# A two-layer MLP behind a dynamic convolution: the fifth product of each slice with 96 stationary columns for 128

## The chip, the core and the metric

The kernel runs on one core of one Trainium2 chip. The metric is the device time of one execution in microseconds (us). The core has five engines: TensorE (PE, with a row of its own for weight loads, PEld), VectorE (DVE), ScalarE (ACT), GpSimd (POOL) and SyncE (SP), which issues most DMAs.

## What is computed

The reference, cut to what matters. A softmax over 7 taps makes weights for a causal convolution along the sequence, in 8 groups of 24 features; its result of 8192 tokens x 192 features goes through two MLPs without biases, 192 to 2048 to 192 each. Everything is in float32; inputs come as float64 bits.

```python
def _attn_ref(x, weight_gen):            # x: 2 x 4096 x 192, weight_gen: 2 x 4096 x 8 x 7
    w = softmax(weight_gen, axis=-1)     # written out in the reference
    x_unf = x_pad[:, idx, :].reshape(B, S, K, H, group)
    out = np.einsum('bshk,bskhg->bshg', w, x_unf)
    return out.reshape(B, S, D)

def _moe_ref(x, w_in, w_out):            # first MLP
    r = np.maximum(x @ w_in, 0.0)
    return (r * r) @ w_out

def _moe2_ref(x, w_in, w_out):           # second MLP
    h = x @ w_in
    return (h * (1.0 / (1.0 + np.exp(-1.702 * h)))) @ w_out
```

## The kernel before

The 8192 tokens are cut into 16 blocks of N = 512; the 2048 hidden features (FF) into 16 slices of 128, which are worked on in 8 pairs, q = 0 to 7. A step is (l, j, q): layer l, block j, pair of slices q. For each step `mm_in` makes the hidden values h of the two slices, ScalarE applies the activation (g), and `mm_out` adds their part of the output into PSUM, where it collects over all q.

To keep float32 precision at the rate of the fp32r type, each operand is split into a high part (rounded to fp32r) and a low part (what is left, again in fp32r), and a product is made as a sum of products of parts. g becomes gh (a cast on ScalarE, line 387) and gl (g - gh, a subtraction on VectorE, line 393). The weights of the second product, `wo`, have for each slice f a row of 2 x 192 columns: high parts of features 0 to 127, then high parts of the 64 features past 128 (at column P = 128), then low parts of these 64 (at 192), then low parts of features 0 to 127 (at C_LA = 256). `SECOND` (line 396) lists the five products of a slice as (output a, first column of wo, part of g):

- (0, 0, 0): gh with the high parts of features 0 to 127, into output 0
- (0, C_LA, 0): gh with their low parts, into output 0
- (1, P, 0): gh with 128 columns from column 128, that is, the high and the low parts of features 128 to 191 side by side, into output 1
- (0, 0, 1): gl with the high parts of features 0 to 127, into output 0
- (1, P, 1): gl with the same 128 columns from 128 on, into output 1; of these only the 64 of the high parts matter, the other 64 are the product of two low parts

Output 1 holds the two halves for the features past 128 on partitions 0 to 63 and 64 to 127; they are added later by a swap through DMA (`t_swap`) and an addition.

In all but the first two blocks of layer 0, a product is issued as two matmuls, on rows 0 to 63 and 64 to 127 of the operands (`HALVES`), into PSUM tiles of their own: p00 and p01 for output 0, p10 and p11 for output 1. These are the forms 64*128. In blocks 0 and 1 of layer 0 (`whole`) it is one matmul on all 128 rows. In the last step of a block, q = 7, the ten products of its two slices are sorted by output, so that output 0 is complete before output 1. `start` marks the matmul that opens a sum in PSUM, `stop` the last.

The order of the work is written out by hand. Steps alternate on PE as mm_in of step n + 2, then mm_out of step n. In each turn of the loop gl is made, then PE's part issued, then the planned side work, then gh. gh and gl have two buffers each. Behind mm_out of a block's last step stands `sum_task`, in which ScalarE copies p00 and p10 (line 431) and VectorE adds p01 and p11 (line 432). `transposed` (line 345) and `t_turn` (line 519) transpose on PE at block borders.

Of the kernel before, what the change touches and what calls it, by code (L numbers as in the profile page):

```python
# [17 lines left out]
def kernel(  # L18
# [15 lines left out]
    P = 128  # L34
# [8 lines left out]
    NF = FF // P  # L43
    NQ = NF // 2
# [30 lines left out]
    wih, wil, wo = [], [], []  # L75
    DM = D - P
# [6 lines left out]
    C_HM, C_LM, C_LA = P, P + DM, P + 2 * DM  # L83
# [281 lines left out]
    p_t = {}  # L365
# [27 lines left out]
        nc.vector.tensor_sub(gl, g, f32(gh))  # L393
        g_t[l, j, q] = gh, gl

    SECOND = [(0, 0, 0), (0, C_LA, 0), (1, P, 0), (0, 0, 1), (1, P, 1)]

    def mm_out(l, j, q):

        g = g_t.pop((l, j, q))  # L400
        whole = l == 0 and j < 2
        parts = [(slice(0, P), j)] if whole else [(HALVES[i], i) for i in range(2)]
        if q == 0:
            p_t[l, j] = {
                (a, i): ps_p.tile([P, N], F32, tag=f"p{a}{i}", name=f"p{a}{i}_{l}_{j}")
                for a in range(2) for _, i in parts
            }
        ops = [(e, o, *op) for e in range(2) for o, op in enumerate(SECOND)]
        if q == NQ - 1:

            ops.sort(key=lambda op: op[2])
        for e, o, a, c, n in ops:
            f = 2 * q + e
            for rows, i in parts:
                nc.tensor.matmul(  # L415
                    out=p_t[l, j][a, i], lhsT=wo[l][rows, f, c:c + P], rhs=g[n][rows, e, :],
                    start=(f == 0 and o in (0, 2)), stop=(f == NF - 1 and o >= 3),
                )

    def sum_task(l, j, hold):  # L420

        def f():
            s = hold["s"] = s_p.tile([P, 2, N], F32, tag="s", name=f"s{l}_{j}")
            p = p_t.pop((l, j))
            if len(p) == 2:
                for a in range(2):
                    nc.scalar.copy(s[:, a, :], p[a, j])
                return
            t = s_p.tile([P, 2, N], F32, tag="s", name=f"t{l}_{j}")
            for a in range(2):  # L430
                nc.scalar.copy(t[:, a, :], p[a, 0])  # L431
                nc.vector.tensor_add(s[:, a, :], p[a, 1], t[:, a, :])  # L432

        return f
# [116 lines left out]
    second_step = [4 * (n // 2) + 6 + n % 2 if n < WHOLE - LAG else 2 * (n + LAG) + 1 for n in range(len(pairs))]  # L551
    steps = {i: (mm_in, n) for n, i in enumerate(first_step)}
    steps |= {i: (mm_out, n) for n, i in enumerate(second_step)}
    assert len(steps) == 2 * len(pairs)
    first, done = {}, {}
# [84 lines left out]
    for s in range(3, TP // SB):  # L640
        i = first[0, s * SB // TB - 1] - 7
        plan(softmax(s), (i - 8, i, i + 1, i + 2, i + 3))
    for n in range(2 * NQ):
        kind = (InChunk, OutChunk)[n % 2]
        i = 4 * NQ + 7.5 + n * 4.0
# [16 lines left out]
    for n, i in enumerate(first_step):  # L662
        i = second_step[n - LAG] if LAG <= n < WHOLE else i + 1
# [3 lines left out]
    with tc.manual_schedule():  # L667
        for i in range(-PRE, 2 * (len(pairs) + LAG) + 8):
# [3 lines left out]
            if i in steps:  # L672
                f, n = steps[i]
# [36 lines left out]
```

## Time and profile before

| | us |
|---|---|
| median of 3 runs | 1166.42 |
| lowest and highest | 1166.27, 1166.82 |
| span of the profiled execution, first to last instruction | 1163.6 |
| median less span | 2.8 |
| PE busy in that span | 1146.5 |
| ACT busy | 780.1 |
| DVE busy | 677.6 |

The profile is of one execution; its span is what its rows add up to, and the time of a run lies some us above it. A busy time is the time in which at least one instruction of the engine runs. Ends of matmuls are modelled, and neighbours overlap, so for PE the distance from start to start says more than a duration. The granted clock is given as a share of full speed.

### The profile page before, as it was taken

To read this page: it belongs to the slowest core of one execution; us is meant where nothing else is said; L and a number is where in the kernel's file an instruction comes from. 1 tells how busy PE (TensorE), PEld (TensorE's weight loads), DVE (VectorE), ACT (ScalarE), POOL (GpSimd) and SP (SyncE) were. 2 spreads that over 40 slices of the span, in tenths; PEclk is the share of its full clock that TensorE was granted. 3 is DMA by queue.
4 is the path that set the end of the run, shared out by engine and by line. 5 is a ranking of instruction groups with operands and counts; after the bars stand their busy time and mean duration, and the time that the engine had idled before them with its cause. 6 is when DMAs were issued, how large, how long until landed. Compare 5 with 4: busy or idle time off the path is not lost.

```text
span 1163.6 us, 23632 instructions
## 1 busy us (share of the span) xinstructions
PE 1146.5 (99%) x10248; PEld 1109.3 (95%) x10248; DVE 677.6 (58%) x792; ACT 780.1 (67%) x851; POOL 17.6 (2%) x26
## 2 busy tenths in 40 slices
PE   6999999999999999999999999999999999999998
PEld 4777899999999999999999999999999999999998
DVE  7998899794564636555474554746455343343342
ACT  3877888876767667675767757677575765555554
POOL 1000010010000000000000000000000000000000
PEclk9999999999999999999999999999999999999999
DMA  8503452532120121210211120121210110110110
GB/s 208 171 1 84 108 143 64 139 76 60 46 62 9 39 58 41 62 37 10 58 50 53 37 60 8 50 58 33 62 37 10 24 42 19 37 37 11 32 37 28
DMA packets 35576, 64.04 MB, mean 55 GB/s; under 512 B 5268, under 2 KB 21138, under 8 KB 35472
## 3 DMA queue, kind: packets, MB, share of 16 engines
q1 hardware_dynamic: 32640, 59.25, 18.3%
q0 software_dynamic: 2304, 3.15, 1.7%
q8 instruction: 80, 1.31, 0.5%
q14 instruction: 24, 0.20, 0.1%
q10 hardware_dynamic: 528, 0.13, 0.0%
HBM read 30.13 MB, written 6.29 MB: 31 GB/s over the span
## 4 chain that ended last, share of the span: by engine, by line
PE 97%; DVE 1%; ACT 1%; DMA 1%; issue 0%; SPq 0%; DVEq 0%
PE p L415 50%; PE h L374 45%; PE tx L345 1%; DMA xt<-in_x_dram 1%; DVE pr L290 1%; PE u L519 0%; PE sumi L107 0%; ACT g L380 0%; DVE xs L325 0%; ACT xs L324 0%; DVE early_us L157 0%; ACT g L381 0%; PE sumo L107 0%; DVE early_us L161 0%; DVE early_us L156 0%
## 5 line engine op out<-in xcount | busy, mean ns | idle before, releaser
L393 DVE TENSOR_TENSOR gl<-g,gh 128x1024 fp32r<-128x1024 f32 x256 | 313.2, 1224 | 327.7 <-ACT gh L387 326.0
L415 PE MATMUL p<-gh,wo 64*128 64x512 f32 (+1 forms) x2976 | 472.0, 387 | 0.6 <-ACT wo L217 0.6
L374 PE MATMUL h<-xs,wih 64*128 64x512 f32 x3072 | 460.3, 389 | 0.4 <-DVE xs L325 0.2
L415 PEld LDWEIGHTS p<-gh,wo 64*128 64x128 f32 (+1 forms) x2976 | 349.6, 184 | 10.1 <-issue 2.5
L374 PEld LDWEIGHTS h<-xs,wih 64*128 64x128 f32 x3072 | 345.0, 184 | 10.3 <-issue 1.8
L415 PE MATMUL p<-gl,wo 64*128 64x512 f32 (+1 forms) x1984 | 354.8, 386 | 0.0
L387 ACT CAST gh<-g 128x1024 fp32r<-128x1024 f32 x256 | 268.7, 1050 | 79.4 <-PE p L415 76.9
L415 PEld LDWEIGHTS p<-gl,wo 64*128 64x128 f32 (+1 forms) x1984 | 236.3, 184 | 4.4
L374 PE MATMUL h<-xs,wil 64*128 64x512 f32 x1536 | 228.9, 387 | 0.1
L383 ACT ACTIVATE g<-h 128x1024 f32<-128x1024 f32 x128 | 131.7, 1029 | 144.8 <-PE h L374 132.2
L380 ACT ACTIVATE g<-h 128x1024 f32<-128x1024 f32 x128 | 131.7, 1029 | 104.5 <-PE h L374 103.0
L374 PEld LDWEIGHTS h<-xs,wil 64*128 64x128 f32 x1536 | 174.5, 184 | 4.3 <-DVE wil L203 0.6
L381 ACT ACTIVATE g<-g 128x1024 f32<-128x1024 f32 x128 | 135.8, 1061 | 4.1
L290 DVE TENSOR_TENSOR pr<-xt,wg 128x768 f32<-128x768 f32 x112 | 104.9, 951 | 2.2 <-DMA xt<-in_x_dram 2.2
L302 DVE TENSOR_TENSOR pr<-pr,pr 128x768 f32<-128x768 f32 x84 | 80.1, 954 | 1.0
L432 DVE TENSOR_TENSOR s<-p,t 128x512 f32<-128x512 f32 x60 | 40.3, 689 | 55.7 <-ACT t L431 55.6
L325 DVE TENSOR_TENSOR xs<-s,xs 128x1024 fp32r<-128x1024 f32 x16 | 19.6, 1226 | 39.5 <-ACT xs L324 39.5
L431 ACT COPY t<-p 128x512 f32<-128x512 f32 x60 | 33.7, 584 | 12.7 <-PE p L415 12.7
L325 DVE TENSOR_TENSOR xs<-tx,xs 128x1024 fp32r<-128x1024 f32 x16 | 19.3, 1204 | 30.0 <-ACT xs L324 30.0
L345 PEld LDWEIGHTS tx<-ident,pr 64*128 64x128 f32 x448 | 19.5, 150 | 12.7 <-DVE pr L290 10.9
L345 PE MATMUL tx<-ident,pr 64*128 64x64 f32 x448 | 19.6, 237 | 10.7 <-DVE pr L290 10.5
L324 ACT CAST xs<-tx 128x1024 fp32r<-128x1024 f32 x16 | 16.2, 1011 | 12.0 <-PE tx L345 11.9
(73 smaller groups left out, 273.1 us busy)
## 6 DMA issues: line engine op xcount, KB each, us to landing
xs<-xs SPq DMA_DIRECT2D x128, 128.0 KB, 2.4
xt<-in_x_dram SPq DMA_DIRECT2D x14, 960.0 KB, 5.0
out_dram<-o SPq DMA_DIRECT2D x15, 384.0 KB, 2.8
w<-s SPq DMA_DIRECT2D x32, 128.0 KB, 2.3
early_raw<-in_moe_w_in_dram SPq DMA_DIRECT2D x16, 192.0 KB, 5.1
early_raw<-in_moe_w_out_dram SPq DMA_DIRECT2D x8, 384.0 KB, 4.0
ri<-in_moe_w_in_dram SPq DMA_DIRECT2D x16, 192.0 KB, 3.5
ro<-in_moe_w_out_dram SPq DMA_DIRECT2D x8, 384.0 KB, 3.2
```

The source lines that it names most:

```text
L290: nc.vector.tensor_mul(pr, hold["x"][:, k:k + TB, :].rearrange("p t (h g) -> p t h g", h=H), wg_t[s][:, t0:t0 + TB, :, k:k + 1].to_broadca ...
L302: nc.vector.tensor_add(hold["p", 0], hold["p", 0], p)
L325: lambda: nc.vector.tensor_sub(lo, src, f32(hi)),
L345: nc.tensor.matmul(out=hold["ps"][:, i, c:c + R], lhsT=cols, rhs=ident[rows, rows], is_transpose=True, start=(first and a == 0 and t == 0) ...
L374: nc.tensor.matmul(out=h[:, i, :], lhsT=w[HALVES[i], q, c, :], rhs=v[HALVES[i], n, PLACE[l][i][c], :], start=(o == 0), stop=(o == len(ops) ...
L380: nc.scalar.activation(out=g, in_=h, func=AF.Relu)
L381: nc.scalar.activation(out=g, in_=g, func=AF.Square)
L383: nc.scalar.activation(out=g, in_=h, func=AF.Gelu_apprx_sigmoid)
L387: nc.scalar.copy(gh, g_t[l, j, q])
L393: nc.vector.tensor_sub(gl, g, f32(gh))
L415: nc.tensor.matmul(out=p_t[l, j][a, i], lhsT=wo[l][rows, f, c:c + P], rhs=g[n][rows, e, :], start=(f == 0 and o in (0, 2)), stop=(f == NF ...
L432: nc.vector.tensor_add(s[:, a, :], p[a, 1], t[:, a, :])
```

## The change

The fifth product of a slice takes 96 stationary columns in place of 128: the 64 high parts and 32 of the 64 low parts. It writes 96 of the 128 partitions of output 1. `SECOND` gets the number of columns as a fourth entry. What it leaves out is the product of gl with the low parts of 32 features. As the last matmul into output 1 in a block should cover all its partitions, the last two products of a block change places, and `start` and `stop` are found from the order. All else is as it was.

```diff
-    SECOND = [(0, 0, 0), (0, C_LA, 0), (1, P, 0), (0, 0, 1), (1, P, 1)]
+    SECOND = [(0, 0, 0, P), (0, C_LA, 0, P), (1, P, 0, P), (0, 0, 1, P), (1, P, 1, DM + P // 4)]
...
-        ops = [(e, o, *op) for e in range(2) for o, op in enumerate(SECOND)]
+        ops = [(e, *op) for e in range(2) for op in SECOND]
         if q == NQ - 1:
 
-            ops.sort(key=lambda op: op[2])
-        for e, o, a, c, n in ops:
+            ops.sort(key=lambda op: op[1])
+            ops[-2:] = ops[:-3:-1]
+        opened, last = set(), {a: n for n, (_, a, *_) in enumerate(ops)}
+        for o, (e, a, c, n, m) in enumerate(ops):
             f = 2 * q + e
             for rows, i in parts:
                 nc.tensor.matmul(
-                    out=p_t[l, j][a, i], lhsT=wo[l][rows, f, c:c + P], rhs=g[n][rows, e, :],
-                    start=(f == 0 and o in (0, 2)), stop=(f == NF - 1 and o >= 3),
+                    out=p_t[l, j][a, i][0:m], lhsT=wo[l][rows, f, c:c + m], rhs=g[n][rows, e, :],
+                    start=(f == 0 and a not in opened), stop=(q == NQ - 1 and o == last[a]),
                 )
+            opened.add(a)
```

On PE, the four products into output 1 at the end of a block (here block 11 of layer 0, q = 7; the names are output tile, part of g and weights, the size that of the output) stood like this before:

```order
L415 MATMUL p10_0_11_7737<-gh0_11_7_8030,wo0_94 128x512
L415 MATMUL p11_0_11_7738<-gh0_11_7_8030,wo0_94 128x512
L415 MATMUL p10_0_11_7737<-gl0_11_7_8032,wo0_94 128x512
L415 MATMUL p11_0_11_7738<-gl0_11_7_8032,wo0_94 128x512
L415 MATMUL p10_0_11_7737<-gh0_11_7_8030,wo0_94 128x512
L415 MATMUL p11_0_11_7738<-gh0_11_7_8030,wo0_94 128x512
L415 MATMUL p10_0_11_7737<-gl0_11_7_8032,wo0_94 128x512
L415 MATMUL p11_0_11_7738<-gl0_11_7_8032,wo0_94 128x512
```

The last product with gl now stands ahead of the last one with gh, so that the two narrow products of the step are neighbours, and gh is read by the block's last two matmuls:

```order
L417 MATMUL p10_0_11_7737<-gh0_11_7_8030,wo0_94 128x512
L417 MATMUL p11_0_11_7738<-gh0_11_7_8030,wo0_94 128x512
L417 MATMUL p10_0_11_7737<-gl0_11_7_8032,wo0_94 96x512
L417 MATMUL p11_0_11_7738<-gl0_11_7_8032,wo0_94 96x512
L417 MATMUL p10_0_11_7737<-gl0_11_7_8032,wo0_94 96x512
L417 MATMUL p11_0_11_7738<-gl0_11_7_8032,wo0_94 96x512
L417 MATMUL p10_0_11_7737<-gh0_11_7_8030,wo0_94 128x512
L417 MATMUL p11_0_11_7738<-gh0_11_7_8030,wo0_94 128x512
```

In all other steps nothing moves. There PE's products of one slice (block 11, q = 3) now read:

```order
L417 MATMUL p00_0_11_7735<-gh0_11_3_7812,wo0_94 128x512
L417 MATMUL p01_0_11_7736<-gh0_11_3_7812,wo0_94 128x512
L417 MATMUL p00_0_11_7735<-gh0_11_3_7812,wo0_94 128x512
L417 MATMUL p01_0_11_7736<-gh0_11_3_7812,wo0_94 128x512
L417 MATMUL p10_0_11_7737<-gh0_11_3_7812,wo0_94 128x512
L417 MATMUL p11_0_11_7738<-gh0_11_3_7812,wo0_94 128x512
L417 MATMUL p00_0_11_7735<-gl0_11_3_7814,wo0_94 128x512
L417 MATMUL p01_0_11_7736<-gl0_11_3_7814,wo0_94 128x512
L417 MATMUL p10_0_11_7737<-gl0_11_3_7814,wo0_94 96x512
L417 MATMUL p11_0_11_7738<-gl0_11_3_7814,wo0_94 96x512
```

The last two rows wrote 128x512 before; the other eight are the same.

## Rows read from the trace of the kernel before

**Rows 1.** The page's head and part 1: span; busy us (share of the span) xinstructions

```profile
span 1163.6 us, 23632 instructions
...
PE 1146.5 (99%) x10248; PEld 1109.3 (95%) x10248; DVE 677.6 (58%) x792; ACT 780.1 (67%) x851; POOL 17.6 (2%) x26
```

**Rows 2.** The chain's shares, by engine and line; then PE's waits: us, times, longest

```profile
PE 97%; DVE 1%; ACT 1%; DMA 1%; issue 0%; SPq 0%; DVEq 0%
PE p L415 50%; PE h L374 45%; PE tx L345 1%; DMA xt<-in_x_dram 1%; DVE pr L290 1%; PE u L519 0%; PE sumi L107 0%; ACT g L380 0%; DVE xs L325 0%; ACT xs L324 0%; DVE early_us L157 0%; ACT g L381 0%; PE sumo L107 0%; DVE early_us L161 0%; DVE early_us L156 0%
...
PE tx L345 <- DVE pr L290: 10.5, 2, 10.4
PE u L476 <- DVE s L432: 0.9, 2, 0.4
```

**Rows 3.** PE's groups by form: xcount | busy us, mean ns of one | idle before

```profile
L374 PE MATMUL h<-xs,wih 64*128 64x512 f32 x3072 | 460.3, 389 | 0.4 <-DVE xs L325 0.2
L415 PE MATMUL p<-gh,wo 64*128 64x512 f32 x2880 | 442.9, 386 | 0.0
L415 PE MATMUL p<-gl,wo 64*128 64x512 f32 x1920 | 334.3, 386 | 0.0
...
L415 PE MATMUL p<-gl,wo 128*128 128x512 f32 x64 | 20.5, 391 | 0.0
L345 PE MATMUL tx<-ident,pr 64*128 64x64 f32 x448 | 19.6, 237 | 10.7 <-DVE pr L290 10.5
```

**Rows 4.** The chain, pieces of 600 to 640 us: start us, us, what

```profile
602.98 2.04 PE h L374 x18
605.01 2.27 PE p L415 x20
607.28 2.04 PE h L374 x18
```

**Rows 5.** Timeline of a block's last step: start us, us, engine line op x [idle before]

```profile
600.27 0.47 PEld L415 LDWEIGHTS p<-gh,wo 64*128 64x128 f32 x4
600.49 0.67 PE L415 MATMUL p<-gh,wo 64*128 64x512 f32 x4
...
600.95 0.44 PE L415 MATMUL p<-gl,wo 64*128 64x512 f32 x2
...
601.17 0.67 PE L415 MATMUL p<-gh,wo 64*128 64x512 f32 x4
...
601.62 0.44 PE L415 MATMUL p<-gl,wo 64*128 64x512 f32 x2
...
602.05 0.59 ACT L431 COPY t<-p 128x512 f32<-128x512 f32 x1 [0.28 <-PE p L415]
...
602.53 0.44 PE L415 MATMUL p<-gl,wo 64*128 64x512 f32 x2
...
602.95 0.59 ACT L431 COPY t<-p 128x512 f32<-128x512 f32 x1 [0.32 <-PE p L415]
...
603.44 1.05 ACT L387 CAST gh<-g 128x1024 fp32r<-128x1024 f32 x1
...
604.52 1.23 DVE L393 TENSOR_TENSOR gl<-g,gh 128x1024 fp32r<-128x1024 f32 x1 [0.26 <-ACT gh L387]
...
609.11 0.90 PE L415 MATMUL p<-gh,wo 64*128 64x512 f32 x6
```

**Rows 6.** Transposes in the timeline; then two stretches: busy (x) by engine, clock, DMA

```profile
33.28 1.30 PE L345 MATMUL tx<-ident,pr 64*128 64x64 f32 x35
...
33.65:34.35 0.70, 0.70 (x28) 0.70 (x26) 0.70 (x2) 0.67 (x2) 0.00 (x0) 1.00 1.10 377
200.00:1000.00 800.00, 800.00 (x7262) 799.20 (x7260) 441.92 (x488) 544.81 (x576) 6.90 (x8) 1.00 0.17 45
```

**Rows 7.** Timeline of PE around products on all 128 rows, and the changes of form

```profile
59.98 0.84 PE L374 MATMUL h<-xs,wil 64*128 64x512 f32 x6
60.66 0.84 PE L374 MATMUL h<-xs,wih 64*128 64x512 f32 x6
61.43 0.97 PE L415 MATMUL p<-gh,wo 128*128 128x512 f32 x3
...
64.53 0.61 PE L415 MATMUL p<-gl,wo 128*128 128x512 f32 x2
64.99 0.84 PE L415 MATMUL p<-gh,wo 128*128 128x512 f32 x3
65.67 0.61 PE L415 MATMUL p<-gl,wo 128*128 128x512 f32 x2
66.21 0.97 PE L374 MATMUL h<-xs,wih 64*128 64x512 f32 x6
```

## The prediction

> **What bounds the kernel now.** I read the totals by engine first [rows 1]: TensorE (PE) is busy 1146.5 of 1163.6 us, its weight loads (PEld) 1109.3, while VectorE and ScalarE stand at 58% and 67%. The chain that ended last says the same [rows 2]: 97% of it is PE, half of it in line 415, the second product, and 45% in line 374, the first. The third view is what PE waited for [rows 2]: 10.4 us for the first convolution sums at the start and then less than 2 us in the whole run. So PE runs without a gap from there on, and the reader is to see that only the time of a PE instruction, not a wait, can move the end.
>
> Then I want the time of one product. A busy sum or a mean duration doesn't give it: the mean of one is 386 to 389 ns [rows 3], but products overlap, so it says nothing of the rate. The rate is in the chain's pieces [rows 4]: each mm_in takes 2.04 us for 18 matmuls and each mm_out 2.27 us for 20. Away from the first two blocks a product is two matmuls, one on each half of the rows, which run side by side; so a piece of mm_out is 10 products in 2.27 us, 227 ns each, and mm_in gives 2.04 / 9 = 227 ns as well. The timeline of one slice shows it for each kind [rows 5]: two products with gh start at 600.49 and the product with gl at 600.95 (230 ns each), the next gh at 601.17 (220 ns later), and five products take 600.49 to 601.62, 226 ns each. A product of gl takes what one of gh takes. The granted clock is 1.00 over 200 to 1000 us [rows 6], the upper level, 2.4 GHz. At one of the 512 moving columns a cycle a product would take 213 ns; so the trace has some 14 ns on each product that are not columns streaming by. What these 14 ns are is the open question here.
>
> **The change part by part.** The fifth product of a slice is counted from the rows by form [rows 3]: 1920 matmuls read gl on half the rows, two to a product, and 64 on all rows, one to a product: 960 + 64 = 1024 products with gl, of which every second is the fifth, 512 in all. At 227 ns they are 116 us, a tenth of the span. One nanosecond on each is 0.51 us. The change gives them 96 stationary columns for 128 and leaves the 512 moving columns as they are.
>
> *The stream of moving columns.* Same count, same clock. No row of before has a stationary operand of other than 128 columns (every form in [rows 3] is 64*128 or 128*128), so the cost of 96 has to be bounded. The nearest evidence is that the other side of the tile, its rows, makes no difference: on 128 rows two products with gl run from 64.53 to 64.99 and three with gh from there to 65.67 [rows 7], 227 to 230 ns each, as on half the rows. I take 0 ns for the stream.
>
> *The weight load.* It is a separate row that runs ahead: the loads for the first products of the slice start at 600.27 and their product at 600.49, so a load has 0.22 us beside the product before it [rows 5]. What it needs is bounded by the transposes, which stream only 64 columns and load 128 for each: 35 of them take 1.30 us [rows 6]; less the last one's own 0.24 us (237 ns, [rows 3]) that is 1.06 us for 17 pairs, 62 ns a pair at clock 1.00. A load of 128 columns therefore fits in 62 ns, and one of 96 can save at most a quarter of that, 16 ns. In the slice about 160 ns of the 0.22 us are spare, so I take 0 here too. If the cover is not what it seems, the gain is bounded by the 14 ns of a product that are not stream: 512 x 13.7 ns = 7.0 us, 1166.4 - 7.0 = 1159.4. If these 14 ns go with the stationary columns, a quarter of them goes: 512 x 3.4 = 1.7 us, 1164.7. From the other side the nearest price of a different form of product is the mean of gl on 128 rows against gl on 64, 391 to 386 ns [rows 3]: 512 x 5 = 2.6 us, 1169.0. Between these ends I take zero, since [rows 5] is the nearest row: the kernel's own product with a load well ahead of it.
>
> One rule speaks for a gain. The Trainium skill, "TensorE: Matmul & The Clock Gate", section "LDWEIGHTS (loading the stationary operand)", gives a load as the stationary columns over 1.2 per ns: about 107 ns for 128 and 80 for 96, 27 ns less. Were that on the path, the estimate by that page would be 512 x 27 = 13.7 us; the transposes' 62 ns a pair do not agree with 107, and the load lies beside a product.
>
> *The last slice of a block.* There the ten products are sorted by output, and the last two change places: the fifth product of the second half comes one earlier, and the last reading of gh one product, 227 ns, later, 32 times (16 blocks, 2 layers). Who waits for gh's buffer is the next copy on ScalarE. In the trace it stands behind the two copies of the sums, which wait for the same last products: they start at 602.05 and 602.95, the copy to gh at 603.44 [rows 5], while the last product starts at 602.53, so 227 ns vanish behind a queue that is busy anyway. Its subtraction on VectorE ends at 605.75, and PE wants the result after the next slice, from 609.11: over 3 us of cover. Cost 0; without any cover 32 x 0.227 = 7.3 us. No DMA and no queue is moved, and the count of instructions on each engine stays.
>
> The sum: span 1163.6 + 0 + 0 + 0 = 1163.6 us. The median of the runs shown is 1166.42, 2.8 us over the span, which lies around it and doesn't depend on the products: **1166.4 us**.
>
> **The rivals.**
> *The 14 ns are the load's tail.* If the last part of a load stands between two products, a narrower one shortens it. For it: 14 ns on each product that the stream doesn't explain, in mm_in, in mm_out and in both tile heights alike, and each has its 128-column load. Against: the load starts 0.22 us ahead and fits in 62 ns. By a quarter of the 14 ns it gives 1164.7, which can't be told from no change; all of it gives 1159.4. It shows as faster from 4.6 ns on each fifth product (2.33 / 512). The Trainium skill, "TensorE: Matmul & The Clock Gate", section "LDWEIGHTS (loading the stationary operand)", stands on this rival's side, as far as it makes the load go with its columns.
>
> *The narrow product is another form, and PE pays at each change of form (slower).* The place is in front of and behind each fifth product. The price is in the trace, where products on all rows alternate with products on half rows [rows 7]: three products of mm_in run from 59.98 to 60.66, 0.68 us, but the three before the change of form from 60.66 to 61.43, 0.77; and the two before the change back from 65.67 to 66.21, 0.54, where two take 0.46. That is 0.08 to 0.09 us a change. A fifth product has one on each side, save where two are neighbours in a block's last slice: 32 x (7 x 4 + 2) = 960 changes x 0.09 = 86 us, 1252 us. Against: all forms that the rows name are 128 columns wide [rows 3], and the two that cost something at a change differ in their rows, which stay as they are here. The Trainium skill, "TensorEngine Tiling (Array Packing)", section "Key Properties", says that a change of tiling mode drains the engine, which agrees with the 0.09 us; none of the modes that it lists is 96 columns wide. A smaller price of this kind (a slower way to load a width that isn't 128, or a partly filled tile) decides from the same 4.6 ns on.
>
> *The change doesn't do what it says on the chip*, that is, a tile of 128 columns is loaded whatever is asked for. Time 1166.4, as forecast; only the load's rows would tell.
>
> **How the numbers follow.** Forecast, no effect to half a microsecond, the undone narrowing among it: 0.62. A quarter of the 14 ns, about 1164.7: 0.13, still within 0.2%. More of it, 1159.4 to 1164: 0.13. Slower through another form, from 5 ns a product to the full 86 us: 0.12, of which half may lie below 1169. A measurement of this kernel can tell about 0.2%, 2.3 us, from no change (1164.1 to 1168.8). So within 0.2% is 0.75, faster 0.13, slower 0.12. The first two cases alone hold less than 8 in 10, so the range goes to the bounds of the unknown price, 1159.4 below and 1169.0 above, and leaves out the dear half of the slower case.
>
> **What would show it.** Right: in the chain, pieces of mm_out still 2.27 us for 20 matmuls; in the timeline the product after a fifth starts 0.23 us behind it; PEclk 1.00; the load rows of the fifth product in a group of their own, 64x96, shorter or not, with PE's busy time unchanged; the copy to gh behind a block's end at the same distance from the sums' copies. Wrong in the first way: pieces of mm_out of 2.24 to 2.26 us, two fifth products a piece shorter by the same few ns, and the span shorter by 256 times the piece's loss. Wrong in the second: pieces of 2.6 us with an added 0.09 us on each side of a fifth product. The forecast falls if the start-to-start time of a product depends on its stationary columns in either direction.

## The result: 1% slower

The changed kernel takes 1178.15 us (median; 1176.88 to 1178.54 in 4 runs), the kernel before in the same session 1166.35: ratio 1.0099 [1.0085, 1.0113], 11.8 us more. The forecast of no change, and the range to 1169.0, are both missed.

The page of the changed kernel, span, totals by engine and shares of the chain:

```profile
span 1175.8 us, 23661 instructions
PE 1158.8 (99%) x10248; PEld 951.6 (81%) x10248; DVE 677.6 (58%) x792; ACT 780.3 (66%) x851; POOL 17.6 (1%) x26
PE 96%; DVE 1%; DMA 1%; ACT 1%; issue 0%; SPq 0%; DVEq 0%; ACTq 0%
```

Against [rows 1, 2] the span is 12.2 us longer, and PE's busy time, 1158.8 for 1146.5, longer by 12.3: all of the loss is on PE, in products and not in a wait. Spread over the 512 narrow products it is 24 ns each.

The groups of PE and PEld by form (mean ns of one behind the comma), those of gl in `mm_out`:

```profile
L417 PE MATMUL p<-gl,wo 64*128 64x512 f32 x960 | 189.3, 385 | 0.0
L417 PE MATMUL p<-gl,wo 64*96 64x512 f32 x960 | 186.2, 389 | 0.0
L417 PEld LDWEIGHTS p<-gl,wo 64*128 64x128 f32 x960 | 92.9, 184 | 17.9
L417 PEld LDWEIGHTS p<-gl,wo 64*96 64x96 f32 x960 | 79.9, 157 | 18.5
```

So the tile does have 96 columns, and its load is shorter, 157 ns for 184. The matmuls' modelled means, 385 and 389, again tell nothing of the rate (answering [rows 3]). The chain does (start us, us, what), from 600 us on:

```profile
604.47 2.06 PE h L374 x18
...
610.88 2.30 PE p L417 x20
613.18 2.06 PE h L374 x18
615.24 2.30 PE p L417 x20
...
626.26 0.50 PE tx L345 x16
626.76 2.13 PE h L374 x18
```

A step took 2.27 + 2.04 us [rows 4] and now takes 2.30 + 2.06. Nearly half of the loss stands in `mm_in`, none of whose products was changed. The timeline of PE over one step shows how it runs on (start us, us, engine line op):

```profile
610.71 0.85 PE L417 MATMUL p<-gh,wo 64*128 64x512 f32 x6
611.39 0.63 PE L417 MATMUL p<-gl,wo 64*128 64x512 f32 x4
611.85 0.87 PE L417 MATMUL p<-gh,wo 64*128 64x512 f32 x6
612.55 0.62 PE L417 MATMUL p<-gl,wo 64*128 64x512 f32 x4
613.01 0.87 PE L374 MATMUL h<-xs,wih 64*128 64x512 f32 x6
613.71 0.85 PE L374 MATMUL h<-xs,wil 64*128 64x512 f32 x6
614.39 0.85 PE L374 MATMUL h<-xs,wih 64*128 64x512 f32 x6
615.07 0.85 PE L417 MATMUL p<-gh,wo 64*128 64x512 f32 x6
```

A row of x6 is three products; the second of the two products in a row of gl (x4) is the narrow one (a row that joins two forms is named by its first). The first three products take 0.68 us, as before. Behind the first narrow product three take 0.70 (611.85 to 612.55), behind the second again 0.70 (613.01 to 613.71), and only then 0.68. Single starts in the trace give the distances from one product to the next, in ns, the first of them the one that leads up to the narrow product: 230, 230, 235, 233, 236, 224, 231, 236, 228, 232, 231, then 226 to 227 until the next step's narrow product. I call 226.7 ns, to which the kernel before keeps, the **settled** distance. The first eleven sum to 2546 ns, 11 settled ones (226.67 ns, to one more digit) to 2493: 53 ns lost in a step. The 12.2 us are 230 such losses, and there are 256 steps.

The windows view from 200 to 1000 us answers [rows 6]: 7181 matmuls for 7262, at the same clock of 1.00.

```profile
200.00:1000.00 800.00, 800.00 (x7181) 665.67 (x7179) 439.62 (x486) 541.39 (x572) 6.87 (x8) 1.00 0.17 45
```

PEld's busy time falls by much more than 512 shorter loads would explain, 665.67 us for 799.20. Single starts show why: in this stretch the two matmuls of a product start 57 or 63 ns apart in the kernel before and mostly 3 to 17 ns apart in the changed one, so more of their loads lie on top of each other. This alone isn't the loss: from 134 to 151 us they start 3 or 4 ns apart in the kernel before too, and its products there are 226.7 ns apart.

### The profile page after: what moved, and what is told of

It is laid out like the page before. It is cut to its first block, busy times and chain, and to the rows that moved or that the text cites. A ratio compares the mean times of both kernels' runs of the same rounds, so it can differ in the third digit from the quotient of the medians.

```text
span 1175.8 us, 23661 instructions
## 1 busy us (share of the span) xinstructions
PE 1158.8 (99%) x10248; PEld 951.6 (81%) x10248; DVE 677.6 (58%) x792; ACT 780.3 (66%) x851; POOL 17.6 (1%) x26
## 4 chain that ended last, share of the span: by engine, by line
PE 96%; DVE 1%; DMA 1%; ACT 1%; issue 0%; SPq 0%; DVEq 0%; ACTq 0%
PE p L417 50%; PE h L374 44%; PE tx L345 1%; DMA xt<-in_x_dram 1%; PE u L522 0%; DVE pr L290 0%; DMA early_raw<-in_moe_w_out_dram 0%; ACT g L380 0%; DVE xs L325 0%; ACT xs L324 0%; DVE early_us L157 0%; ACT g L381 0%; SPq L192 0%; SPq L332 0%; DVE early_us L161 0%
## 5 line engine op out<-in xcount | busy, mean ns | idle before, releaser
L417 PE MATMUL p<-gh,wo 64*128 64x512 f32 (+1 forms) x2976 | 451.4, 390 | 0.6 <-ACT wo L217 0.6
L374 PE MATMUL h<-xs,wih 64*128 64x512 f32 x3072 | 440.9, 391 | 0.6 <-ACT g L380 0.3
L417 PEld LDWEIGHTS p<-gh,wo 64*128 64x128 f32 (+1 forms) x2976 | 295.2, 184 | 66.0 <-issue 2.5
L374 PEld LDWEIGHTS h<-xs,wih 64*128 64x128 f32 x3072 | 293.1, 184 | 62.0 <-issue 1.6
L417 PE MATMUL p<-gl,wo 64*128 64x512 f32 (+1 forms) x1984 | 325.7, 388 | 0.0
L374 PE MATMUL h<-xs,wil 64*128 64x512 f32 x1536 | 218.8, 388 | 0.1
L417 PEld LDWEIGHTS p<-gl,wo 64*128 64x128 f32 (+1 forms) x1984 | 183.9, 171 | 39.2
L374 PEld LDWEIGHTS h<-xs,wil 64*128 64x128 f32 x1536 | 148.1, 184 | 29.6 <-DVE wil L203 0.6
L324 ACT CAST xs<-tx 128x1024 fp32r<-128x1024 f32 x16 | 16.2, 1010 | 12.2 <-PE tx L345 12.2
```

Source lines behind the costliest of these rows:

```text
L374: nc.tensor.matmul(out=h[:, i, :], lhsT=w[HALVES[i], q, c, :], rhs=v[HALVES[i], n, PLACE[l][i][c], :], start=(o == 0), stop=(o == len(ops) ...
L417: nc.tensor.matmul(out=p_t[l, j][a, i][0:m], lhsT=wo[l][rows, f, c:c + m], rhs=g[n][rows, e, :], start=(f == 0 and a not in opened), stop= ...
```

## The experiments

All times in us, medians; the kernel before is that of the same session. "Loss" is the difference of the two.

| kernel | before | this | ratio [95%] | loss |
|---|---|---|---|---|
| order_only | 1165.97 | 1165.83 | 1.0000 [0.9991, 1.0010] | -0.1 |
| moving_496 | 1165.97 | 1163.28 | 0.9976 [0.9966, 0.9985] | -2.7 |
| second_96 | 1165.97 | 1180.01 | 1.0119 [1.0104, 1.0134] | 14.0 |
| narrow_112 | 1165.97 | 1174.91 | 1.0076 [1.0061, 1.0091] | 8.9 |
| narrow_half | 1166.10 | 1178.04 | 1.0103 [1.0086, 1.0120] | 11.9 |
| narrow_shifted | 1166.10 | 1165.91 | 0.9996 [0.9986, 1.0005] | -0.2 |
| narrow_124 | 1166.10 | 1166.06 | 0.9999 [0.9990, 1.0009] | 0.0 |
| narrow_80 | 1166.10 | 1175.53 | 1.0079 [1.0064, 1.0094] | 9.4 |
| wide_earlier | 1166.11 | 1172.14 | 1.0053 [1.0038, 1.0068] | 6.0 |
| second_96_end | 1166.11 | 1166.15 | 1.0003 [0.9994, 1.0012] | 0.0 |
| moving_by_64 | 1166.11 | 1175.55 | 1.0084 [1.0069, 1.0099] | 9.4 |
| all_by_64 | 1166.11 | 1166.44 | 1.0003 [0.9994, 1.0013] | 0.3 |
| moving_by_32 | 1166.11 | 1196.65 | 1.0259 [1.0244, 1.0274] | 30.5 |
| moving_by_96 | 1166.11 | 1196.90 | 1.0262 [1.0245, 1.0279] | 30.8 |
| narrow_second | 1166.11 | 1177.57 | 1.0096 [1.0081, 1.0111] | 11.5 |

### Which part of the change it is

**order_only**: the change with all its order and flags, but 128 columns.

```diff
-    SECOND = [(0, 0, 0, P), (0, C_LA, 0, P), (1, P, 0, P), (0, 0, 1, P), (1, P, 1, DM + P // 4)]
+    SECOND = [(0, 0, 0, P), (0, C_LA, 0, P), (1, P, 0, P), (0, 0, 1, P), (1, P, 1, P)]
```

> The order of the change (last two products of a block exchanged, start and stop taken from the order) with all five products at 128 columns. Theory A (the narrow stationary operand disturbs the rhythm of the products that follow it, some 25 ns for each narrow product, about 12 us in all): 1166.4 us, the time of before, and products 226.7 ns apart throughout. Rival B (the narrow product has a price of its own, at its own place): 1166.4 as well. Rival C (the later last reading of gh at the end of a block costs it): up to 32 x 0.227 = 7.3 us more, or the whole 12 us.

No loss. The exchange of the last two products is innocent; all of it is the narrow tile.

**moving_496**: the kernel before, its fifth product on 496 of the 512 moving columns.

```diff
-                    out=p_t[l, j][a, i], lhsT=wo[l][rows, f, c:c + P], rhs=g[n][rows, e, :],
+                    out=p_t[l, j][a, i][:, 0:N if o != 4 else 496], lhsT=wo[l][rows, f, c:c + P], rhs=g[n][rows, e, 0:N if o != 4 else 496],
```

> The fifth product at 128 stationary columns but with 496 of its 512 moving columns; 16 tokens of its term in each block are left out. It takes 16 / 2.4 = 6.7 ns less of the stream by itself, 512 x 6.7 = 3.4 us. If any product that departs from the rhythm disturbs the ones behind it as a narrow one does (25 ns each): 1166.4 - 3.4 + 12 = about 1175, with distances of 230 to 236 ns behind it. If only the stationary width matters: 1163.0, with 226.7 ns behind it.

```profile
601.70 2.04 PE h L374 x18
603.74 2.25 PE p L415 x20
```

In the chain the piece of `mm_out` falls to 2.25 and `mm_in` keeps 2.04. The shortened products take 220 ns, 16 columns less at 2.4 GHz (6.7 ns) with the same 14 ns on top, and their neighbours stay settled. (512 times 6.7 ns are 3.4 us; the 2.7 measured have an interval of 1.7 to 4.0.) An odd product in the sequence is therefore not enough to make a loss.

### How the loss depends on the number of narrow products

**narrow_half** and **narrow_second**: only one of a step's two fifth products is narrow. The text on record of narrow_half calls it the second slice's; the edit narrows that of the first slice (e = 0), and narrow_second that of the second.

The line that goes, then that of narrow_half and that of narrow_second:

```diff
-        ops = [(e, *op) for e in range(2) for op in SECOND]
+        ops = [(e, *op[:3], P if e else op[3]) for e in range(2) for op in SECOND]
+        ops = [(e, *op[:3], op[3] if e else P) for e in range(2) for op in SECOND]
```

> Only the second slice's fifth product is narrow (96 columns), 256 of them in place of 512; the narrow product then stands behind each step's last gl product, ahead of mm_in, and the ten products of the next step are back at 227 ns. Theory A (each narrow product throws the products behind it out of their distance of 226.7 ns for about six products, 25 ns in sum, and then it is over): 256 x 25 = 6.4 us, 1172.4, with mm_out's first five products undisturbed. Rival B (the price is at the narrow product itself): also some 6 us, but in the narrow product's own distance and not in the following mm_in. Rival E (it takes only a few narrow products to keep the kernel in a slower state): near 1178.

> The counterpart of the run that made one fifth product in two narrow. That run's kernel narrows the first slice's fifth product of each step (its expectation names the second by mistake) and lost the whole 12 us: 53 ns a step, settled again only eleven products later, so that the second narrow product of the changed kernel falls into unsettled products and adds nothing. Here only the second slice's is narrow. If a narrow product in settled products always costs the same settling: 1178 again, with 230, 230, 235, 233, 236 and 224 ns behind it and the rest in mm_in. If the price depends on its place in the step: about half, 1172.

Either alone costs what both cost (11.9 and 11.5 us against 11.8). The distances behind the first slice's narrow product are those of the changed kernel one by one, though five products later a 128-column tile stands where a narrow one stood. So one product of 96 columns sets off some eleven uneven distances, and a second one within them adds nothing. In narrow_second's chain the loss has moved nearly whole into the piece that the change didn't touch:

```profile
602.40 2.27 PE p L417 x20
604.68 2.09 PE h L374 x18
```

### Width, or place

**narrow_112**, **narrow_124**, **narrow_80**: the changed kernel with another width for its fifth product, from the same first column.

```diff
-    SECOND = [(0, 0, 0, P), (0, C_LA, 0, P), (1, P, 0, P), (0, 0, 1, P), (1, P, 1, DM + P // 4)]
+    SECOND = [(0, 0, 0, P), (0, C_LA, 0, P), (1, P, 0, P), (0, 0, 1, P), (1, P, 1, 112)]
```

The other two have 124 and 80 in its place.

> The fifth product with 112 stationary columns in place of 96. If the loss goes with the columns that are missing (32 before, 16 here): half of 12 us, 1172.3. If any width that isn't 128 costs the same: 1178. If 112 still counts as 128 (a tile in whole groups of 32 columns): 1166.4.

> The fifth product with 124 columns. 112 columns lost 8.9 us and 96 columns 12. If the loss grows with the missing columns and bends (112 took 75% of it), 4 missing columns give 2 to 4 us: 1168 to 1170. If any width other than 128 throws the products out of their distance for six products: 9 us or more, 1175. If only a multiple of 8 or 16 below 128 counts: 1166.

> The fifth product with 80 columns, 16 fewer than in the change. If the loss grows with the missing columns: 1180 to 1184. If every width that isn't 128 costs about one recovery of 25 ns: 1178, the same as with 96. If widths beyond one more group of 16 lie better with the neighbours (as the distances of 224 ns hint): below 1178.

124 columns cost nothing, 112 cost 8.9 us, 96 11.8 and 80 9.4: a narrower tile isn't a dearer one, and a partly filled tile isn't dear as such. At 112 and 80 the sequence settles sooner. Most of their narrow products have four uneven distances behind them, 236, 228, 233 and 231 ns, some 20 ns in sum over settled ones, and each of a step's two pays them, where at 96 columns the two share one run of eleven and 53 ns. In narrow_112's timeline the three products behind a narrow one take 0.69 us (615.43 to 616.12, 616.58 to 617.27), and the next three are settled again at 0.68:

```profile
614.97 0.62 PE L417 MATMUL p<-gl,wo 64*128 64x512 f32 x4
615.43 0.85 PE L417 MATMUL p<-gh,wo 64*128 64x512 f32 x6
616.12 0.62 PE L417 MATMUL p<-gl,wo 64*128 64x512 f32 x4
616.58 0.85 PE L374 MATMUL h<-xs,wih 64*128 64x512 f32 x6
617.27 0.84 PE L374 MATMUL h<-xs,wil 64*128 64x512 f32 x6
617.95 0.62 PE L374 MATMUL h<-xs,wih 64*128 64x512 f32 x4
```

**second_96**: all five products of a slice at 96 columns, the first 96 of each 128, save the products that open and close a sum.

```diff
-    SECOND = [(0, 0, 0, P), (0, C_LA, 0, P), (1, P, 0, P), (0, 0, 1, P), (1, P, 1, DM + P // 4)]
+    SECOND = [(0, 0, 0, 96), (0, C_LA, 0, 96), (1, P, 0, 96), (0, 0, 1, 96), (1, P, 1, 96)]
         for o, (e, a, c, n, m) in enumerate(ops):
+            if (q == 0 and a not in opened) or (q == NQ - 1 and o == last[a]):
+                m = P
```

> All five second products of a slice at 96 columns, except the one that opens and the one that closes each sum in PSUM (4 of 160 in a block and layer); a quarter of the second product is left out. Theory A (a change of width disturbs, a constant width doesn't): inside a step the ten narrow products run at a constant distance again, and there are two changes of width in a step (to narrow and back) where the change has four; about half of the 12 us or less, 1169 to 1173. Rival B (each narrow product costs 24 ns by itself): 2560 - 128 = 2432 narrow products, 58 us more, 1225. Rival D (the distance of products goes down with the columns, and only the changes cost): below 1166, pieces of 20 matmuls under 2.27 us.

Nearly five times as many narrow products (2432 for 512) cost 14.0 us, hardly more than the change. None of the theories had that: not a price for each narrow product, not one for each change of width (there are two in a step here, four in the changed kernel). Within `mm_out` the distance goes round 230, 232, 228, 230 (230.0 in the mean). Where `mm_in`'s 128 columns come back, eight uneven ones follow, 233, 236, 224, 231, 236, 228, 233 and 231, which are those of the changed kernel from its fourth on, within 1 ns. Its chain:

```profile
629.71 2.31 PE p L419 x20
632.02 2.07 PE h L374 x18
```

That left one thing that goes with narrowing and isn't the width: where the columns lie. The first 96 columns from column 128 on end at column 224, 32 columns or 128 bytes of a partition earlier than the 128 do. In the kernel before every product's columns end a whole multiple of 128 columns (512 bytes) behind the start of its weights, since `wo` has 384 to a slice and its blocks begin at 0, 128 and 256.

**narrow_shifted**: 96 columns from column 160 on, so that they end at 256 where the 128 ended.

```diff
-    SECOND = [(0, 0, 0, P), (0, C_LA, 0, P), (1, P, 0, P), (0, 0, 1, P), (1, P, 1, DM + P // 4)]
+    SECOND = [(0, 0, 0, P), (0, C_LA, 0, P), (1, P, 0, P), (0, 0, 1, P), (1, P + P // 4, 1, DM + P // 4)]
```

> The fifth product with 96 columns that end where the 128 ended, from column 160 of wo on in place of 128: 32 high and 64 low parts of the features past 128 (wrong ones, so the output differs). Theory A (it is the count of columns that disturbs): 1178, as with the first 96. Rival F (it is where the load reads, its first or last address against that of the products around it): another time, 1166 if the end of the 128 is what matters.

No loss at all; its chain is the kernel before's again, with 960 loads of 96 columns in it:

```profile
602.99 2.04 PE h L374 x18
605.03 2.27 PE p L417 x20
```

**second_96_end**: second_96, but the last 96 of each 128 columns; the diff is against second_96.

```diff
-                    out=p_t[l, j][a, i][0:m], lhsT=wo[l][rows, f, c:c + m], rhs=g[n][rows, e, :],
+                    out=p_t[l, j][a, i][0:m], lhsT=wo[l][rows, f, c + P - m:c + P], rhs=g[n][rows, e, :],
```

> As the run with all second products at 96 columns, but each takes the last 96 of its 128 columns in place of the first 96; a quarter of the second product is left out. Theory F (the place of the end): every load ends where it ended before, 1166, 226.7 ns throughout, with 2432 narrow products. Theory A (the count): 1180, as with the first 96.

14.0 us go to 0.0. The timeline of PE shows narrow products at the settled distance, in rows of three products (x6) and of two (x4); the first row also holds products of 128 columns that open a sum:

```profile
605.27 0.94 PE L419 MATMUL p<-gh,wo 64*128 64x512 f32 x6
605.95 0.71 PE L419 MATMUL p<-gl,wo 64*96 64x512 f32 x4
606.40 0.94 PE L419 MATMUL p<-gh,wo 64*96 64x512 f32 x6
607.08 0.71 PE L419 MATMUL p<-gl,wo 64*96 64x512 f32 x4
```

Three take 0.68 us, two 0.45 to 0.46. So 96 columns for 128 cost nothing and gain nothing by their number, and **the place of the columns is what the change paid for**. 124 columns, which end 16 bytes earlier, are the one earlier end that stayed free.

**wide_earlier**: the kernel before, its fifth product on 128 columns that begin 32 earlier (96 to 223, ending where the change's 96 end).

```diff
-                    out=p_t[l, j][a, i], lhsT=wo[l][rows, f, c:c + P], rhs=g[n][rows, e, :],
+                    out=p_t[l, j][a, i], lhsT=wo[l][rows, f, c - 32 * (o == 4):c - 32 * (o == 4) + P], rhs=g[n][rows, e, :],
```

> All products at 128 columns; the fifth product's 128 columns begin 32 earlier (column 96 of wo, not 128), so that they end where the change's 96 end. The output differs. The run with the 96 columns that end where the 128 had ended lost nothing, so theory F is now the leading one: what disturbs is where a load's columns end in memory against the loads around it, not how many there are. Theory F: 1178, with the distances of the changed kernel (230, 230, 235, 233, 236, 224 ns behind each). Theory A (count of columns, and the shifted run was an exception): 1166.2.

A full tile loses too, so the sign is right, but only 6.0 us, half of the change's loss, and in another pattern: 233 and 234 ns around each fifth product (13.7 ns in sum over settled ones; 512 times that are 7.0 us), then settled at once. `mm_in` loses nothing:

```profile
603.86 2.29 PE p L415 x20
606.15 2.04 PE h L374 x18
```

So the place of the end isn't the whole rule. The tile's start and width differ from the change's, and so does the distance between the two matmuls of a product, 37 ns here and mostly 3 to 17 in the changed kernel; which of these makes the difference is open.

### The other side: where the moving operand lies

If the place against the moving operand matters, moving the moving operands (g's parts and xs) against all weights must cost something with no tile narrowed, and moving everything together nothing. **moving_by_64**, **moving_by_32**, **moving_by_96**: the kernel before with unused bytes between the weights and all that is allocated behind them. **all_by_64**: 64 bytes ahead of the weights, so that these and the moving operands move alike.

The diff is that of moving_by_64 (16 floats); moving_by_32 has 8 and moving_by_96 has 24.

```diff
     w_p = [ctx.enter_context(tc.tile_pool(name=f"w{l}", bufs=1)) for l in range(2)]
+    gap_p = ctx.enter_context(tc.tile_pool(name="gap", bufs=1))
     wg_p = ctx.enter_context(tc.tile_pool(name="wg", bufs=2))
...
+    gap = gap_p.tile([P, 16], F32, name="gap")
```

all_by_64 puts it into the pool of constants, which lies ahead of the weights:

```diff
+    gap = const.tile([P, 16], F32, name="gap")
```

> The kernel before with 64 bytes of unused memory between the weights and everything behind them, so that xs, gh and gl (the moving sides) lie 64 bytes higher in each partition and the weights stay. If the disturbance comes of load and moving side meeting in memory, then a constant offset between them may have a distance of products of its own: some per cent up or down, 1155 to 1185 (a constant stream of 96 columns had 230 ns, 17 us over all products). If only a load's place against the other loads counts: 1166.2.

> The kernel before with 64 bytes of unused memory ahead of the weights, so that weights and moving sides lie 64 bytes higher alike. If the place of a load's end in memory counts by itself (theory F, absolute): another constant distance of products, 1155 to 1185. If only the places relative to one another count: 1166.2.

> As the run with the moving sides 64 bytes higher, but 32 bytes. That run had a steady cycle of 229, 232 and 226 ns, 229.0 in the mean, and cost 9.4 us. If the distance of products follows the offset between load and moving side, 32 bytes give a third value: up to 1175, or below 1166 if part of the 14 ns that a product takes over its 512 columns comes of the same meeting. If only offsets of whole 64 bytes count: 1166.2.

> The moving sides 96 bytes higher. If what counts repeats every 64 bytes: the time of 32 bytes. If the distance grows with the offset: above 1175. If there is an offset at which load and moving side don't meet: below 1166.

An unused tile between two buffers costs 9.4 us at 64 bytes and 30.5 and 30.8 us, 2.6%, at 32 and 96, though the instructions differ in nothing but addresses; 32 bytes go far beyond the 1175 us that their text on record allowed. Ahead of the weights 64 bytes cost nothing. At 32 bytes all of it is PE's busy time again, 1177.0 us for 1146.5, and PE waits no longer than before. The chains of moving_by_64 (first two rows), and of moving_by_32:

```profile
603.64 2.06 PE h L376 x18
605.70 2.29 PE p L417 x20
```

```profile
604.19 2.10 PE h L376 x18
606.28 2.33 PE p L417 x20
```

With a constant offset all products are at a constant mean distance: 226.7 ns without the gap, 228.9 at 64 (mostly going round 229, 232, 226), 233.3 at 32 and at 96. None of these settles to 226.7; every product has the offset. 96 costs what 32 does, but 64 isn't free as 0 is, so what counts doesn't simply repeat every 64 bytes. **At 64 bytes it is the place of the moving operands (and of what is allocated with them) against the weights that counts, not their place as such.** No run moves both sides by 32 or 96, so for these it isn't shown: buffers that lie off whole multiples of 64 bytes may be dear by themselves.

## Why the prediction was wrong

**The bound** was right: PE, by the time of its instructions. The loss is where the prediction said that a loss would have to be.

**The stream at 0 ns** was right for the number of columns. 2432 products of 96 columns cost 0.0 us (second_96_end), within the interval's 1.4 us above and 0.7 below, under 0.6 ns each.

**The last slice's order at 0** was right: order_only, -0.1 us.

**The weight load at 0 is the step that failed.** It was measured at 24 ns for each fifth product in the mean, and is paid as 53 ns once a step; the upper bound that the prediction drew was 5 ns, from 391 against 386 ns of modelled means [rows 3], of which it had itself said that they tell nothing of the rate. The step asked how long a load takes and how much cover it has. Its answer holds as far as the load got shorter (157 ns for 184) and a shorter one changed nothing; the spare 160 ns do not stand, since load rows of 184 ns leave some 40 of the 0.22 us. It didn't ask what the load reads and from where. "[rows 5] is the nearest row" was no bound: each of its loads ends a whole multiple of 512 bytes behind the start of its weights, as all in the kernel before do, so the row contained nothing of the thing that the change moved. The diff had it: `c:c + m` for `c:c + P` keeps the first column and moves the last one.

There was also a row that showed the settled distance to be a state that can be lost. In the chain of the kernel before, behind the transposes that a block needs:

```profile
615.89 2.04 PE h L374 x18
...
620.20 0.44 PE tx L345 x13
620.65 2.19 PE h L374 x18
622.84 2.27 PE p L415 x20
```

That `mm_in` takes 2.19 us for 2.04. 0.09 of the excess lies between its first two products (318 ns, read on their second matmuls), a price like that of [rows 7]; but from its second product on the trace has 231, 236, 228, 232, 231, 227 ns, the very distances with which the changed kernel comes to rest. The prediction read such places only as a price of 0.08 to 0.09 us paid once. In the changed kernel the same place takes 0.50 + 2.13 us (above), 2.63 as here (0.44 + 2.19), with the same distances one by one: where the sequence is broken anyway, the narrow product ahead of it costs `mm_in` nothing more.

**The rivals.** *The 14 ns are the load's tail*: wrong. Tiles of 96 columns take the same 226.7 ns (narrow_shifted, second_96_end), and 16 moving columns less leave the 14 ns whole (moving_496). The Trainium skill's rule beside it ("TensorE: Matmul & The Clock Gate", section "LDWEIGHTS (loading the stationary operand)") gives, as an estimate by its formula, 27 ns less for 96 columns than for 128 (80 for 107); the trace agrees on the difference of the load rows, 184 - 157 = 27 ns, though not on their length, and none of it reached the distance of products. *Another form, paid at each change*: right in sign, wrong in mechanism. No step of 0.09 us stands at a narrow product, and its smaller variant, a dear width or partly filled tile, falls with second_96_end. Its 0.12 was too little, above all for a reason that the prediction had written down: no row of before had such a tile. *The change doesn't do what it says*: wrong, the load rows are 64x96.

**What would show it.** The test "the product after a fifth starts 0.23 us behind it" would have passed: that distance is 230 ns. The loss lies in ten more distances of up to 9 ns over the settled one, and ends far behind the product that a reader would look at. Pieces of the chain, which the prediction named too, do show it; `mm_in`'s piece, which it didn't name, shows nearly as much of it as `mm_out`'s.

**What stays open.** That place decides is shown by pairs that differ in nothing else (second_96 and second_96_end; the changed kernel and narrow_shifted; moving_by_64 and all_by_64). Why it does, in the memory or in PE's reading of it, no run shows. Nor why 96 columns cost twice what 128 with the same end cost, why the sequence settles after four distances at 112 and 80 and after eleven at 96, why 16 bytes (124) are free, what the 14 ns of a settled product are, or whether a gap other than 0, 32, 64 and 96 bytes gives less than 226.7 ns; others weren't tried. No run beats the kernel before except moving_496, which leaves moving columns out: a narrow tile at the right place gains nothing (narrow_shifted, second_96_end).

## What to carry to other kernels

Fewer stationary columns (96 for 128) didn't shorten products that stream 512 columns back to back, so such a cut had nothing to win, and it lost where the slice that is kept ended elsewhere in memory. In a kernel that PE bounds, take the distance from one product to the next, look in the trace for places where it isn't constant, and ask of an edit not only how long an operation takes but which addresses it reads against those of the operand beside it. A change in allocation alone (an unused tile of 32 or 96 bytes) cost 2.6% here, more than twice the loss of the edit in question, so hold the layout still while another edit is measured.

## What the runs showed of the hardware that was not expected

- The distance of back-to-back products depends on the place of the stationary operand against the moving one: 226.7 ns at the offset of the kernel before, 228.9 with 64 bytes more, 233.3 with 32 or 96 more, and 226.7 again where both sides are moved by 64. (No run moved both by 32 or 96.)
- One load that ends 128 bytes earlier than the others (96 columns) makes some eleven distances of 224 to 236 ns, 53 ns in sum, and a second such load within them adds nothing. One that ends 64 or 192 bytes earlier (112 or 80 columns) makes four of 228 to 236 ns, some 20 ns in sum. One that ends 16 bytes earlier (124 columns) has no effect.
- The last five of the eleven follow in the kernel before behind the transposes (231, 236, 228, 232, 231 ns), so they are not peculiar to narrow tiles.
- The two matmuls of a product start 57 or 63 ns apart in the kernel before from 200 us on and mostly 3 to 17 in the changed kernel; the settled distance of products is 226.7 ns at 3 ns as at 57.
- 96 stationary columns for 128, at the same end, change the distance by less than 0.6 ns in 2432 products.
